# Chunked gated linear attention before two MLPs: a different order of work in each chunk, and other PSUM banks for three of its products

## The chip, the cores and the metric

The kernel runs on one core of a Trainium2 chip. The metric is device time in microseconds (us) from one launch, the median of several runs. Engines are named as in the profile: PE (TensorE matmul), PEld (its weight loads), DVE (VectorE), ACT (ScalarE), POOL (GpSimd), SP (SyncE, which issues all DMAs here).

## The reference

Three stages on float32 data with batch B=4, sequence S=768, model width 384 (8 heads of 48):

```python
f = sigmoid(f_logit)                       # gate per head, token and key channel
state = f[t] * state + k[t] outer v[t]     # per batch and head, 48 x 48
y[t]  = q[t] @ state                       # attention output, 768 tokens
x  = y with heads joined                   # (4, 768, 384)
u  = x + ((x.T @ U) @ V).T                 # token mixing of rank 32
x2 = u + relu(u @ w_ch1) @ w_ch2           # first MLP, 384 -> 1536 -> 384
h  = relu(x2 @ w_in)                       # second MLP, 384 -> 1024
out = (h * sigmoid(conv3(h))) @ w_out      # depthwise conv over the tokens, kernel 3
```

The weights arrive as 64-bit floats and are converted on the chip.

## The kernel before

**Attention.** The recurrence is computed in 24 chunks of 128 tokens, six for each batch. For chunk g, `gate_max(g)` (POOL from chunk 4 on) and `gates(g)` (two ACT passes, exp and ln, in tile `sp`) give the log gates. `prefix(g)` sums them over the tokens with a triangular matmul into tile `n` (PSUM bank 6). ACT makes `a` = exp(-n) and `b` = exp(n) from it; `qh` = q*a and `kh` = k*min(b, limit) follow on POOL (the latter in the inner function `k_hat`). `transposes(g)` turns `qh` and `kh` (banks 1 and 0) and ACT copies them to `qT` and `kT`. `scores(g)` multiplies them into `s` (banks 2 and 3), `mask` applies the causal mask on DVE (tiles `p0`, `p1`). `out_chunk(g)` adds the products `y<-qT,w` (query times state) and `y<-p,v` in bank 4, then forms the chunk's own state product `kv` in bank 7. `state_end(g)` folds `kv` into the running state `w` (DVE `wtmp`, POOL `w`) with the chunk's last gate row, which goes through DRAM (`ends`, `ends_back`).

**Back to tokens and token mixing.** `out_evac(g)` (ACT) copies `y` to `u32`, which is laid out by channel. `tokens(g)` transposes it back to tokens into tile `xt`, also in bank 4; ACT casts it to `xh`, DVE computes the rest `xl` from `xt` and `xh`. `mix_in` adds both into `z` (bank 5). Once a batch is complete, `mix_z` and six calls of `mix_out` (a matmul into a tile `mix` of bank 7 or 6, then a DVE addition into `u32`, row `u`) follow, spread over the chunks of the next batch: in a batch's chunks 3, 4, 5 and, for the batch after, 0, two where the chunk's number i is odd, else one.

**Weight conversion in the gaps.** A weight piece is loaded as raw 64-bit words (`raw`, two buffers), converted in five DVE steps (lines 114 to 118; tiles `cvt`, `cvg`), cast on ACT and completed by a subtraction on POOL. `stage()` issues the load of the next piece, `slot(n)` runs the next n steps. The first pieces are U, the two halves of V (rows `raw<-in_moe_V`), and the convolution weights; 12 pieces of the first MLP's weights follow.

**Order.** The schedule is written out by hand (`manual_schedule`): each engine executes its instructions in program order, and the tile framework adds the waits. A tile in a bank waits for the last reader of the tile that was there before. In each iteration i of the chunk loop PE gets `s(i)`, `n(i+2)`, `z(i-2)`, `xt(i-1)`, the transposes of `qh(i+1)` and `kh(i+1)`, `mix`, `y(i)`, `kv(i)`. DVE gets `wtmp(i-1)`, three conversion steps, both masks, `xl(i-1)`, two conversion steps, `u`. ACT gets the copy of `y(i-1)`, exp and ln of `gates(i+3)`, a weight cast, `a(i+2)`, `xh(i-1)`, `b(i+2)`, the copies of `qT(i+1)`, `kT(i+1)`. POOL gets `w(i-1)`, the weight subtraction, `qh(i+2)`, `b`, `kh(i+2)` and `gate_max(i+4)`. In the first three iterations `gates` runs at the iteration's end. SP issues the loads of `k`, `q`, `f`, `v`, then `ends_back`, one raw piece and `ends`.

**MLPs.** After chunk 23 two MLPs run on PE with each operand split in a high and a low part; the rest of the weight pieces is converted meanwhile. The program ends with a branch on a flag (`tc.If`, line 846) to a fallback that is not taken in these runs.

Of the kernel before, what the change touches and what calls it, by code (L numbers as in the profile page):

```python
# [9 lines left out]
F32 = mybir.dt.float32  # L10
F32R = mybir.dt.float32r
I32 = mybir.dt.int32
# [3 lines left out]

DECAY_LIMIT = 40.0
N_EARLY = 12
SLOT = (3, 2)
EARLY_GATES = 4  # L20
WARM_UP = (8, 5)
FILL_FROM = 22
O_BUFS = 6
SPLIT_FROM = 3
# [7 lines left out]
def kernel(  # L32
# [60 lines left out]

    def w64_load(pool, pairs, p, n):
        raw = pool.tile([128, 2 * 384], I32, tag="raw", name="raw")
        for r0, r1, shape, src in pairs:
            dst = raw[r0:r1, 0:2 * n]
            if shape:  # L100
                dst = dst.rearrange("p (a x) -> p a x", a=shape)
            nc.sync.dma_start(out=dst, in_=src)
        return raw, p, n
# [47 lines left out]
    def mlps(ms, banks, pieces, late, extra):  # L151
# [234 lines left out]
        while done < len(units):  # L386
            down2(*units[done][1:])
            done += 1
            yield

# [12 lines left out]
    def bank(i, shape, name):  # L405
        return banks.tile(shape, F32, tag=f"k{i}", name=name)
# [13 lines left out]

    def heads(t):
        return t.rearrange("p a (j x) -> p (a j) x", j=2)[:, :, 0:D]

    ft, qt, kt, vt = {}, {}, {}, {}
    sps = {}
# [55 lines left out]
    def ends(g):  # L481
        nc.sync.dma_start(out=ends_d[g], in_=a_t[g % 3][127:128].rearrange("o p d -> o (p d)"))
# [4 lines left out]

    qT, kT, sc, pt = {}, {}, {}, {}

    def transposes(g):  # L490
        for src, dst, nm in ((q_t[g % 2], qT, "qT"), (k_t[g % 3], kT, "kT")):
            ps = bank(0 if nm == "kT" else 1, [MP, NP, C], nm + "p")
            for p in range(NP):
                nc.tensor.transpose(out=ps[:, p, :], in_=src[:, p, 0:MP], identity=ident)
            t = (wk1 if nm == "kT" else wk2).tile([MP, NP, C], F32, tag=nm, name=nm)
            nc.scalar.copy(out=t, in_=ps)
            dst[g] = t

    def scores(g):
        kk, qq = kT.pop(g), qT[g]  # L500
# [8 lines left out]
    def mask(g, j):  # L509
        t = wk1.tile([128, NP, C], F32, tag=f"p{j}", name=f"p{j}")  # L510
        nc.vector.tensor_tensor(  # L511
            out=t, in0=sc[g][j], in1=tri.unsqueeze(1).to_broadcast([128, NP, C]), op=ALU.mult
        )
        pt[g].append(t)
# [27 lines left out]
    def strips(parts, started):  # L542
        rounds = [[] for _ in range(4)]
        for part in parts:
            rounds[part[0]].append(part)
        while any(rounds):
            for q in rounds:
                if q:
                    c, dst, lhsT, rhs = q.pop(0)
                    mm(dst, lhsT, rhs, c not in started, False)  # L550
                    started.add(c)

    def out_chunk(g):
        yt[g] = ps = bank(4, [128, KD, C], "y")
        qq, vv, pp = qT.pop(g), vt[g], pt.pop(g)
        parts = []

        def add(gr, lhsT, rhs):
            m, c = divmod(gr, 4)
            parts.append((c, ps[32 * c:32 * (c + 1), m, :], lhsT, rhs))  # L560

        if g % NCH:
            w = w_t[g % 2]
            for p in range(NP):
                for x in range(3):
                    add(3 * p + x, w[:, p, 32 * x:32 * (x + 1)], qq[:, p, :])
        for x, gr, j in ((0, 0, 0), (1, 1, 0), (2, 1, 1), (3, 2, 1)):
            for p in range(NP):
                e = 128 * p + 32 * x
                add(3 * p + gr, vv[:, e:e + 32], pp[j][:, p, :])  # L570
        strips(parts, set())
        if (g + 1) % NCH:
            strips(state(g), set())
        vt.pop(g)
# [3 lines left out]
    def out_evac(g):  # L578
        nc.scalar.copy(out=u32[:, :, g * C:(g + 1) * C], in_=yt.pop(g))

    def tokens(g):
        ps = bank(4, [128, DM], "xt")
        for m in range(KD):
            nc.tensor.transpose(out=ps[:, m * 128:(m + 1) * 128], in_=u32[:, m, g * C:(g + 1) * C], identity=ident)
        h_ = wk1.tile([128, DM], F32R, tag="xh", name="xh")
        l_ = wk1.tile([128, DM], F32R, tag="xl", name="xl")
        nc.scalar.copy(out=h_, in_=ps)
        xh[g], xl[g] = h_, l_
        return lambda: sub(nc.vector, l_, ps, h_.bitcast(F32))
# [69 lines left out]
    with tc.manual_schedule():  # L659
# [5 lines left out]
        )  # L665
        nc.vector.memset(one, 1.0)
        nc.vector.memset(ga, 1.0)
        nc.vector.memset(a_t[0], 1.0)
        nc.vector.memset(q_t[0], 0.0)
        nc.vector.memset(k_t[0], 0.0)  # L670
        for t in v_t:
            nc.gpsimd.memset(t[:, 0:NP * 128].rearrange("p (a x) -> p a x", a=NP)[:, :, D:VO], 0.0)
        for t, x in ((q_t[1], 0.0), (k_t[1], 0.0), (a_t[1], 1.0), (k_t[2], 0.0), (a_t[2], 1.0),
                     (w_t[0], 0.0), (w_t[1], 0.0)):
            nc.gpsimd.memset(t, x)
        for dst, src, nm, g in (
            (ft, f_logit, "f", 0), (kt, k, "k", 0), (qt, q, "q", 0), (ft, f_logit, "f", 1),
            (ft, f_logit, "f", 2), (kt, k, "k", 1), (qt, q, "q", 1), (vt, v, "v", 0),
# [61 lines left out]
        mask(0, 0)  # L740
        mask(0, 1)
        gate_max(3)
        transposes(1)
        prefix(2)()
        gates(3)
        slot(5)
        out_chunk(0)
        load(ft, f_logit, "f", 4)
        load(kt, k, "k", 3)
        load(qt, q, "q", 3)  # L750
        load(vt, v, "v", 2)
        load(vt, v, "v", 3)
        ends(1)
        ends(2)
        ends_back(1)
        slot(1)
        for i in range(1, NG):
# [6 lines left out]
                load(vt, v, "v", i + 3)  # L764
            if i + 1 < NG:
                ends_back(i + 1)
            out_evac(i - 1)
            scores(i)
            if i % NCH:
                state_end(i - 1)  # L770
            if EARLY_GATES <= i and i + 3 < NG:
                gates(i + 3)
            follow = slot_end()
            if 1 < i < FILL_FROM:
                slot(SLOT[0])
            mask(i, 0)
            k_hat = prefix(i + 2) if i + 2 < NG else None
            if i > 1:
                mix_in(i - 2)
            x_low = tokens(i - 1)  # L780
            mask(i, 1)
            x_low()
            if k_hat:
                k_hat()
            for step in follow:
                step()
            if i + 1 < NG:
                transposes(i + 1)
            if i < EARLY_GATES:
                gate_max(i + 3)  # L790
                gates(i + 3)
# [5 lines left out]
                ends(i + 2)  # L797
            if i == FILL_FROM + 1:
                next(mlp)
            if i > 1 and (i - 1) % NCH == 0:  # L800
                b = (i - 1) // NCH - 1
                late_work.append(mix_z(b))
                mixq += [(b, x) for x in range(2 * KD)]
            elif (i - 1) % NCH > 1:
                for at in (7, 6) if i % 2 else (7,):
                    if mixq:
                        mix_out(*mixq.pop(0), at)
            out_chunk(i)
            while tail_work:
                tail_work.pop(0)()  # L810
            if i == FILL_FROM + 1:
# [8 lines left out]
            if i == FILL_FROM:  # L820
                assert not (steps or ready or late_work)
                ls.close()
                mlp = mlps(ms, banks, wq, late, extra)
                next(mlp)
        while mixq:
            mix_out(*mixq.pop(0))
        out_evac(NG - 1)
        mix_in(NG - 2)
        tokens(NG - 1)()
        next(mlp)  # L830
# [170 lines left out]
```

## Time and profile before

| what | us |
|---|---|
| median of 3 runs (lowest to highest) | 678.66 (678.36 to 680.11) |
| the profiled execution, its own time | 681.33 |
| its span, first to last instruction | 679.6 |
| attention, chunk 0's scores to the first MLP matmul | 12.9 to 167.5 |
| busy over the span: PE, DVE, ACT, POOL | 648.3, 441.5, 278.1, 168.4 |

Busy time of PE counts matmuls that wait in its pipeline, so a share near 100% does not say that nothing can be gained. A time in a row is counted from the span's start. The mean granted TensorE clock is 0.993 of full speed.

### The profile page before, as it was taken

What the parts mean: (1) busy time and instruction counts of PE and PEld (TensorE: products, weight loads), DVE (VectorE), ACT (ScalarE), POOL (GpSimd) and SP (SyncE); (2) the same over time, 40 slices, a digit from 0 to 9 for tenths busy, and PEclk for the clock granted to TensorE, in tenths of its full rate; (3) what the DMA queues carried; (4) which work ended last, traced back from release to release, by engine and by line L of the source; (5) the groups of instructions that cost most, each with busy time, mean ns of one, the idle gap of its engine ahead of it and who ended that gap; (6) DMA issues with size and microseconds to landing.
All of it is one profiled execution on the core that took longest, in us unless ns stands there. A gap on an engine that the chain in (4) does not pass through costs nothing.

```text
span 679.6 us, 13505 instructions
## 1 busy us (share of the span) xinstructions
PE 648.3 (95%) x5564; PEld 621.7 (91%) x5564; DVE 441.5 (65%) x697; ACT 278.1 (41%) x554; POOL 168.4 (25%) x202
## 2 busy tenths in 40 slices
PE   7869898989999999999999999999999999999996
PEld 6767777778999999999999999999999999999995
DVE  5658989966899786666211241114898787777763
ACT  5647777764332232123111221113544644553542
POOL 2646778774132131113000020002020120120000
PEclk9979999999999999999999999999999999999999
DMA  8788898841143222210000000000000100100102
GB/s 177 144 163 178 173 202 175 167 84 49 48 139 94 71 70 70 55 62 1 1 0 1 1 1 1 0 1 2 0 1 1 70 1 0 70 1 1 69 1 75
DMA packets 126922, 41.18 MB, mean 61 GB/s; under 512 B 113300, under 2 KB 124076, under 8 KB 126852
## 3 DMA queue, kind: packets, MB, share of 16 engines
q1 hardware_dynamic: 126852, 40.24, 25.3%
q8 instruction: 45, 0.74, 0.4%
q14 instruction: 25, 0.20, 0.1%
HBM read 35.46 MB, written 4.77 MB: 59 GB/s over the span
## 4 chain that ended last, share of the span: by engine, by line
PE 71%; DVE 14%; POOL 4%; ACT 3%; issue 3%; DMA 2%; SPq 2%; POOLq 0%; DVEq 0%; ACTq 0%
PE a L69 33%; PE b L69 32%; PE y L69 3%; DVE cvt L115 2%; DMA q<-in_q_dram 2%; DVE cvg L118 2%; DVE cvg L117 1%; DVE cvt L116 1%; POOL qh L463 1%; DVE cvt L114 1%; PE s L69 1%; DVE p L511 1%; SPq L438 1%; DVE rl L206 1%; DVE xl L72 1%
## 5 line engine op out<-in xcount | busy, mean ns | idle before, releaser
L206 DVE SCALAR_TENSOR_TENSOR rl<-a,rh 128x384 fp32r<-128x384 f32 x96 | 52.6, 556 | 138.3 <-ACT rh L202 138.0
L202 ACT ACTIVATE rh<-a 128x384 fp32r<-128x384 f32 x96 | 47.2, 492 | 219.4 <-PE a L69 219.4
L69 PE MATMUL a<-uh,w1h 128*128 128x384 f32 x288 | 96.6, 336 | 1.0 <-DVE rl L206 1.0
L69 PE MATMUL a<-ul,w1h 128*128 128x384 f32 x288 | 96.6, 335 | 0.0
L69 PE MATMUL b<-rh,w2h 128*128 128x384 f32 x288 | 96.3, 334 | 0.0
L69 PE MATMUL a<-uh,w1l 128*128 128x384 f32 x288 | 96.2, 334 | 0.0
L69 PE MATMUL b<-rh,w2l 128*128 128x384 f32 x288 | 96.2, 334 | 0.0
L69 PE MATMUL b<-rl,w2h 128*128 128x384 f32 x288 | 96.2, 334 | 0.0
L72 POOL TENSOR_TENSOR ul<-u,uh 128x384 fp32r<-128x384 f32 x18 | 23.0, 1298 | 196.2 <-ACT uh L91 196.2
L69 PE MATMUL b<-woh,w1h 128*128 128x384 f32 x264 | 70.9, 337 | 0.0
L69 PEld LDWEIGHTS a<-uh,w1h 128*128 128x128 f32 x288 | 54.1, 188 | 1.9 <-DVE rl L206 1.7
L69 PEld LDWEIGHTS a<-ul,w1h 128*128 128x128 f32 x288 | 54.1, 188 | 0.6 <-DVE ul L72 0.6
L256 ACT ACTIVATE c<-c 128x768 f32<-128x768 f32 x31 | 26.3, 848 | 69.2 <-DVE c L286 69.2
L69 PEld LDWEIGHTS b<-rh,w2h 128*128 128x128 f32 x288 | 54.1, 188 | 0.3 <-issue 0.2
L69 PEld LDWEIGHTS a<-uh,w1l 128*128 128x128 f32 x288 | 54.1, 188 | 0.0
L69 PEld LDWEIGHTS b<-rl,w2h 128*128 128x128 f32 x288 | 54.1, 188 | 0.0
L69 PEld LDWEIGHTS b<-rh,w2l 128*128 128x128 f32 x288 | 54.1, 188 | 0.0
L69 PE MATMUL a<-w2h,winh 128*128 128x384 f32 x192 | 48.8, 335 | 0.0
L69 PEld LDWEIGHTS b<-woh,w1h 128*128 128x128 f32 x264 | 48.1, 188 | 0.0
L69 PE MATMUL b<-wol,w1h 128*128 128x384 f32 x132 | 44.4, 336 | 0.0
L248 ACT ACTIVATE h<-a 128x384 f32<-128x384 f32 x64 | 30.4, 495 | 24.3 <-PE a L69 24.0
L280 DVE TENSOR_SCALAR c<-h,cw 128x768 f32<-128x768 f32 (+1 forms) x33 | 24.2, 734 | 22.8 <-ACT h L248 22.7
(129 smaller groups left out, 1381.1 us busy)
## 6 DMA issues: line engine op xcount, KB each, us to landing
raw<-in_moe_w_ch_dram SPq DMA_DIRECT2D x24, 384.0 KB, 3.1
f<-in_f_logit_dram SPq DMA_DIRECT2D x24, 192.0 KB, 4.9
k<-in_k_dram SPq DMA_DIRECT2D x24, 192.0 KB, 3.2
q<-in_q_dram SPq DMA_DIRECT2D x24, 192.0 KB, 4.6
v<-in_v_dram SPq DMA_DIRECT2D x48, 96.0 KB, 3.4
out_dram<-o SPq DMA_DIRECT2D x24, 192.0 KB, 1.9
raw<-in_moe_w_in_dram SPq DMA_DIRECT2D x8, 384.0 KB, 3.3
raw<-in_moe_w_out_dram SPq DMA_DIRECT2D x8, 384.0 KB, 3.4
```

The costliest lines, as they stand in the source:

```text
L69: nc.tensor.matmul(out=out, lhsT=lhsT, rhs=rhs, start=start, stop=stop, skip_group_check=True)
L72: eng.tensor_tensor(out=out, in0=a, in1=b, op=ALU.subtract)
L114: lambda: ve.tensor_scalar(out=t, in0=hi, scalar1=3, scalar2=0x3FFFFFFF, op0=ALU.logical_shift_left, op1=ALU.bitwise_and),
L115: lambda: ve.scalar_tensor_tensor(out=t, in0=hi, scalar=-(1 << 30), in1=t, op0=ALU.bitwise_and, op1=ALU.bitwise_or),
L116: lambda: ve.scalar_tensor_tensor(out=t, in0=lo, scalar=29, in1=t, op0=ALU.logical_shift_right, op1=ALU.bitwise_or),
L117: lambda: ve.tensor_scalar(out=g, in0=hi, scalar1=0x7FF00000, scalar2=None, op0=ALU.bitwise_and),
L118: lambda: ve.scalar_tensor_tensor(out=w, in0=g, scalar=LEAST_NORMAL, in1=t.bitcast(F32), op0=ALU.is_ge, op1=ALU.mult),
L202: nc.scalar.activation(out=rh[:, hf], in_=ps, func=ACTF.Relu)
L206: nc.vector.scalar_tensor_tensor(out=rl[:, hf], in0=ps, scalar=0.0, in1=rh[:, hf].bitcast(F32), op0=ALU.max, op1=ALU.subtract,)
L248: nc.scalar.activation(out=h[:, 1 + hf.start:1 + hf.stop], in_=ps, func=ACTF.Relu)
L256: nc.scalar.activation(out=c, in_=c, func=ACTF.Sigmoid)
L280: nc.vector.tensor_scalar(out=c[:, s], in0=h[:, t0 + 1:t1 + 1], scalar1=cw[:, J2 + jc[0]:J2 + jc[0] + 1], scalar2=None, op0=ALU.mult)
```

## The change

- `tokens` writes `xt` into bank 0; the transposes of `qh` and `kh` share bank 1 (new function `turn`).
- In each iteration the order is: `state_end(i-1)`, `prefix(i+2)` (PE `n`, ACT `a`, POOL `qh`), `scores(i)`, `k_hat` (ACT `b`, POOL `b`, `kh`), `gates(i+3)`, two conversion steps, `mix_in`, both masks, `tokens(i-1)`, the turn of `qh(i+1)`, `xl`, three conversion steps, `mix_out` (now bank 6), `out_chunk(i)`, `out_evac(i)`, a second `mix_out` in bank 0 where i is odd, and last the turn of `kh(i+1)`.
- One more call of `stage()` ahead of the loop: each raw piece is fetched one piece earlier, with three buffers for `raw` until the MLPs begin. The second half of V is then issued behind the loads that follow chunk 0.
- At the start only the columns between the heads are filled in the `qh`, `kh` and `a` tiles (`between`); the two `w` tiles are filled by DVE instead of POOL. Seven warm-up matmuls instead of eight before the first prefix.
- After the last product of the second MLP, 16 matmuls are issued whose result nobody reads.

```diff
-SLOT = (3, 2)
+SLOT = (2, 3)
-WARM_UP = (8, 5)
+WARM_UP = (7, 5)
...
+    raw_bufs = [3]
-        raw = pool.tile([128, 2 * 384], I32, tag="raw", name="raw")
+        raw = pool.tile([128, 2 * 384], I32, tag="raw", name="raw", bufs=raw_bufs[0])
...
+        flat = w2h.rearrange("p j x -> p (j x)")
+        ps = [bank(i, [128, 512], "wide") for i in range(2)]
+        for n, turns in ((512, 1), (384, 1), (384, 2), (256, 1)):
+            for i in range(4):
+                mm(ps[i % turns][:, 0:n], flat[:, 128 * i:128 * (i + 1)], flat[:, 0:n], turns > 1 or i == 0, False)
...
+    def between(t):
+        return t.rearrange("p a (j x) -> p (a j) x", j=2)[:, :, D:64]
...
+    def turn(g, nm):
+        src, dst = (q_t[g % 2], qT) if nm == "qT" else (k_t[g % 3], kT)
+        ps = bank(1, [MP, NP, C], nm + "p")
+        for p in range(NP):
+            nc.tensor.transpose(out=ps[:, p, :], in_=src[:, p, 0:MP], identity=ident)
+        t = (wk1 if nm == "kT" else wk2).tile([MP, NP, C], F32, tag=nm, name=nm)
+        nc.scalar.copy(out=t, in_=ps)
+        dst[g] = t
...
     def tokens(g):
-        ps = bank(4, [128, DM], "xt")
+        ps = bank(0, [128, DM], "xt")
...
-        nc.vector.memset(a_t[0], 1.0)
-        nc.vector.memset(q_t[0], 0.0)
-        nc.vector.memset(k_t[0], 0.0)
+        for t, x in ((a_t[0], 1.0), (q_t[0], 0.0), (k_t[0], 0.0)):
+            nc.vector.memset(between(t), x)
+        for t in w_t:
+            nc.vector.memset(t, 0.0)
...
-        transposes(1)
+        turn(1, "qT")
...
         out_chunk(0)
+        out_evac(0)
+        turn(1, "kT")
...
         load(vt, v, "v", 3)
+        stage()
         ends(1)
...
-            out_evac(i - 1)
-            scores(i)
             if i % NCH:
                 state_end(i - 1)
+            k_hat = prefix(i + 2) if i + 2 < NG else None
+            scores(i)
+            if k_hat:
+                k_hat()
...
-            mask(i, 0)
-            k_hat = prefix(i + 2) if i + 2 < NG else None
             if i > 1:
                 mix_in(i - 2)
+            mask(i, 0)
+            mask(i, 1)
             x_low = tokens(i - 1)
-            mask(i, 1)
+            if i + 1 < NG:
+                turn(i + 1, "qT")
             x_low()
-            if k_hat:
-                k_hat()
...
-            if i + 1 < NG:
-                transposes(i + 1)
...
+            late_mix = []
...
-                for at in (7, 6) if i % 2 else (7,):
-                    if mixq:
-                        mix_out(*mixq.pop(0), at)
+                if mixq:
+                    mix_out(*mixq.pop(0), 6)
+                if mixq and i % 2:
+                    late_mix.append(mixq.pop(0))
             out_chunk(i)
+            out_evac(i)
+            for m in late_mix:
+                mix_out(*m, 0)
+            if i + 1 < NG:
+                turn(i + 1, "kT")
...
+                raw_bufs[0] = 2
...
-        out_evac(NG - 1)
```

## Rows read from the trace of the kernel before

**Rows 1.** Windows between `scores`: length, busy PE, PEld, DVE, ACT, POOL, clock, DMA share.
```profile
30.16:43.46 13.30, 7.41 (x127) 6.50 (x120) 4.32 (x9) 5.48 (x12) 5.19 (x9) 0.81 0.83 163
...
50.27:74.48 24.21, 21.42 (x429) 18.02 (x422) 21.45 (x39) 18.76 (x42) 17.10 (x23) 1.00 0.87 178
74.48:112.15 37.67, 34.27 (x671) 28.27 (x665) 34.44 (x62) 26.84 (x58) 29.12 (x38) 1.00 0.88 184
112.15:118.92 6.77, 6.30 (x129) 5.06 (x122) 6.57 (x12) 4.62 (x10) 4.97 (x7) 1.00 0.88 187
118.92:125.12 6.20, 5.82 (x129) 4.87 (x121) 5.30 (x10) 3.66 (x9) 5.21 (x7) 1.00 0.69 149
125.12:130.88 5.76, 5.74 (x97) 4.64 (x89) 5.37 (x11) 4.04 (x9) 4.85 (x7) 1.00 0.85 169
130.88:136.42 5.54, 5.29 (x100) 4.18 (x96) 4.87 (x9) 4.72 (x10) 3.68 (x6) 1.00 0.88 177
136.42:142.61 6.19, 5.57 (x127) 4.74 (x120) 5.44 (x10) 4.65 (x11) 4.33 (x6) 1.00 0.90 167
142.61:149.85 7.24, 5.56 (x127) 4.77 (x119) 3.72 (x7) 5.17 (x12) 5.80 (x8) 1.00 0.32 49
149.85:167.53 17.68, 16.57 (x333) 14.04 (x327) 12.66 (x27) 8.49 (x19) 8.48 (x12) 1.00 0.16 47
```

**Rows 2.** Waits of PE, 0 to 215 us: total, times, longest.
```profile
PE y L69 <- DVE xl L72: 10.3, 11, 5.0
PE y L69 <- POOL qh L463: 5.5, 5, 1.7
```

**Rows 3.** Timeline of chunks 2 and 3, all engines.
```profile
27.57 1.00 POOL L463 TENSOR_TENSOR qh<-q,a 128x384 f32<-128x384 f32 x1 [2.36 <-DMA q<-in_q_dram]
...
32.17 0.91 PE L69 MATMUL n<-sp,tri 128*128 128x384 f32 x2 [0.85 <-ACT sp L454]
...
33.42 1.37 SPq L102 DMA_DIRECT2D raw<-in_moe_V_dram  x3
...
36.59 0.57 DVE L114 TENSOR_SCALAR cvt<-raw 96x384 int32<-96x384 int32 x1 [5.47 <-DMA raw<-in_moe_V_dram]
...
39.68 1.51 PE L69 MATMUL y<-qT,w 112*32 112x128 f32 x24 [5.04 <-DVE xl L72]
```

**Rows 4.** Groups of POOL instructions, chunks 9 to 20: busy, mean ns.
```profile
L469 POOL TENSOR_TENSOR kh<-k,b 128x384 f32<-128x384 f32 x12 | 13.2, 1099 | 1.0
...
L467 POOL TENSOR_SCALAR b<-b 128x384 f32<-128x384 f32 x12 | 7.3, 612 | 1.0
```

**Rows 5.** Timeline of the start, all engines.
```profile
3.69 1.88 DVE L446 TENSOR_SCALAR sp<-f 128x384 f32<-128x384 f32 x1 [1.00 <-DMA f<-in_f_logit_dram]
...
20.84 1.00 POOL L463 TENSOR_TENSOR qh<-q,a 128x384 f32<-128x384 f32 x1 [0.39 <-DMA q<-in_q_dram]
```

**Rows 6.** Timeline of chunk 1's prefix sums and the ACT instructions behind them.
```profile
11.99 0.91 PE L69 MATMUL n<-sp,tri 128*128 128x384 f32 x2 [0.17 <-ACT sp L454]
...
13.00 0.49 ACT L462 ACTIVATE a<-n 128x384 f32<-128x384 f32 x1
...
14.89 0.58 ACT L496 COPY qT<-qTp 112x512 f32<-112x512 f32 x1
```

**Rows 7.** Groups of DVE instructions, chunks 9 to 20: busy, mean ns.
```profile
L118 DVE SCALAR_TENSOR_TENSOR cvg<-cvg,cvt 128x384 f32<-128x384 int32 x10 | 8.2, 822 | 0.3
...
L72 DVE TENSOR_TENSOR xl<-xt,xh 128x384 fp32r<-128x384 f32 x12 | 6.6, 551 | 2.1 <-ACT xh L587 1.9
...
L117 DVE TENSOR_SCALAR cvg<-raw 128x384 int32<-128x384 int32 x9 | 5.0, 559 | 0.1
```

**Rows 8.** The end: chain that ended last, then line 846's semaphore instructions.
```profile
660.50 12.51 PE b L69 x72
...
L846 SPq EVENT_SEMAPHORE  x8: 17/17/17, 677.5 to 678.2; - x8
...
L846 PEldq EVENT_SEMAPHORE  x1: 51/51/51, 673.9 to 673.9; - x1
```

More of the change, by code (lines that the diff above doesn't have):

```diff
@@ L488 @@
     qT, kT, sc, pt = {}, {}, {}, {}
-    def transposes(g):
[L491 to L497, printed above, removed]
+    def turn(g, nm):
[6 more added lines that the diff above has]
+        dst[g] = t
+    def transposes(g):
+        turn(g, "qT")
+        turn(g, "kT")
     def scores(g):
@@ L555, in out_chunk, with part @@
         qq, vv, pp = qT.pop(g), vt[g], pt.pop(g)
-        parts = []
-        def add(gr, lhsT, rhs):
+        started = set()
+        def part(gr, lhsT, rhs):
             m, c = divmod(gr, 4)
-            parts.append((c, ps[32 * c:32 * (c + 1), m, :], lhsT, rhs))
+            return c, ps[32 * c:32 * (c + 1), m, :], lhsT, rhs
         if g % NCH:
             w = w_t[g % 2]
[L564 to L571, printed above, removed]
+            strips([part(3 * p + x, w[:, p, 32 * x:32 * (x + 1)], qq[:, p, :])
+                    for p in range(NP) for x in range(3)], started)
+        strips([part(3 * p + gr, vv[:, 128 * p + 32 * x:128 * p + 32 * (x + 1)], pp[j][:, p, :])
+                for x, gr, j in ((0, 0, 0), (1, 1, 0), (2, 1, 1), (3, 2, 1)) for p in range(NP)], started)
         if (g + 1) % NCH:
@@ L667 @@
         nc.vector.memset(ga, 1.0)
-        nc.vector.memset(a_t[0], 1.0)
-        nc.vector.memset(q_t[0], 0.0)
-        nc.vector.memset(k_t[0], 0.0)
+        for t, x in ((a_t[0], 1.0), (q_t[0], 0.0), (k_t[0], 0.0)):
+            nc.vector.memset(between(t), x)
+        for t in w_t:
+            nc.vector.memset(t, 0.0)
         for t in v_t:
             nc.gpsimd.memset(t[:, 0:NP * 128].rearrange("p (a x) -> p a x", a=NP)[:, :, D:VO], 0.0)
-        for t, x in ((q_t[1], 0.0), (k_t[1], 0.0), (a_t[1], 1.0), (k_t[2], 0.0), (a_t[2], 1.0),
-                     (w_t[0], 0.0), (w_t[1], 0.0)):
-            nc.gpsimd.memset(t, x)
+        for t, x in ((q_t[1], 0.0), (k_t[1], 0.0), (a_t[1], 1.0), (k_t[2], 0.0), (a_t[2], 1.0)):
+            nc.gpsimd.memset(between(t), x)
         for dst, src, nm, g in (
```

## The prediction

> **What bounds the kernel now.** I read the windows first, cut at each start of `scores` [rows 1]. The attention stage is PE's, but with gaps: chunks 15 to 20 take 6.77, 6.20, 5.76, 5.54, 6.19 and 7.24 us, while PE is busy 5.3 to 6.3 us in each. Chunk 3 alone takes 13.30 us, at a mean clock of 0.81. In chunks 9 to 14 DVE is busy 34.44 of 37.67 us and the DMA engines 0.88 of the time, so two other resources stand close behind PE. Chunk 20 (7.24 us) has DVE busy only 3.72: not DVE's load but a chain of waits costs 1.68 us there (7.24 - 5.56).
>
> The waits [rows 2] name the chain: `y` stood behind `xl` for 10.3 us, and 5.5 us more are put down to POOL `qh`, which `y` doesn't read and which runs at about the time of `xl`; I count them with `xl`. `y(i)` takes bank 4 from `xt(i-1)`, and `xl` is `xt`'s last reader. Then the timeline of chunk 3 [rows 3]: V's second half is issued at 33.42, DVE waits 5.47 us for it, the masks and `xl` queue behind, and PE stands 5.04 us before `y`.
>
> After 167.5 us the MLPs keep PE filled until 673 us; nothing of their order changes. An earlier end of attention moves them as a whole.
>
> **The change, part by part.**
>
> *V earlier, chunks 1 to 4.* DVE's wait of 5.47 us goes. What is late next is the loop through the gates: `n` first in each iteration means that `s(i)` now queues on PE behind an `n(i+2)` that, in iterations 1 to 3, waits for `gates(i+2)`, ended late in the iteration before. Before, the scores ran ahead of that wait. V's three issues (1.37 us [rows 3]) also move ahead of chunk 4's loads on SP, so q(4), which POOL already waited 2.36 us for until 27.57, comes at about 28.9. From there: `qh` 1.0, `b` 0.6, `kh` 1.1 [rows 4], `gate_max` 0.5 (taken as a little under `b`), exp and ln 1.15 (an estimate, the larger part of the 1.89 in which ACT starts and works off `a`, `b`, exp and ln [rows 6]): `n(5)` at 33.3 instead of 32.17, and chunk 3's scores 0.8 behind it at 34.1 instead of 30.16. The same loop gives the next `n`: 0.95 from `n` to `a`, 0.49, 1.0, 0.6, 1.1, 0.5, 1.15, and some 0.5 of hand-offs make 6.3, so `n(6)` at 39.6 and chunk 4's scores at 40.5 (43.46 before). From chunk 4 on `gates` is out of this loop. Chunk 4 then takes 5.6 (PE's work in a chunk without mixing is 5.57 [rows 1]) instead of 6.81 (43.46 to 50.27): scores of chunk 5 at 46.1. **Gain 4.2.** Bounds: 0 if the loads of q(5), q(6), f(7) come as late as before and everything waits for them; 8.3 if chunk 3 takes 6.2 and chunk 4 5.6.
>
> *The start.* The first `gate_max` takes 1.88 us on DVE while POOL fills tiles [rows 5]; shorter fills can give 1.3 of it back. But `qh(3)` at 20.84 waits for its q load, whose place on SP doesn't change. I take 0, and 1.3 as the other bound. One warm-up matmul less is inside that wait: 0.
>
> *Chunks 5 to 8* (24.21 us, no mixing yet). `y` no longer waits for `xl`; PE's busy 21.42 is the lower bound. The DMA share 0.87 would pass 0.93 at 22.6, and DVE has 21.45 of work. **Gain 1.0**, bounds 0 and 2.5.
>
> *Chunks 9 to 19.* Two things oppose each other. Without the wait for `xl`, a batch's chunk 1 goes from 6.19 to 5.5, chunk 2 from 7.2 to 6.3 (5.56 of PE's work and some 0.7 in which `y<-p,v` waits for masks, since DVE comes late from the first step of `mix_z`): -0.7, -0.7, -0.9 for chunks 13, 19 and 14. But `mix` now always takes bank 6, whose next tile is `n(i+3)`, first on PE in the next iteration, and its reader `u` is DVE's last instruction of the iteration: behind `n` queue `s`, `z`, `xt`, `y` on PE and `a`, `b`, the gates and `xh` on ACT. The loop is: `u` to `n` 0.1; `n` 0.91 and a hand-off to `a`, 0.95; ACT until the gates are done 1.89 [rows 6]; a weight cast in five of six iterations, as long as `a`, 0.4 in the mean; `xh` 0.49; `xl` 0.55; on average 2.5 conversion steps (the sixth place in six is the cast's) of 0.56 to 0.82, taken as 0.64, 1.6; `u` 0.55 like `xl` [rows 7]. Sum 6.53, taken as 6.5. It closes eight times (chunks 9 to 12 and 15 to 18), where the mean was (6.77 + 6.20 + 5.76 + 5.54)/4 = 6.07 [rows 1]: +3.4. **Net +1.1.** Bounds: -5 if DVE reaches `u` before PE is ready for `n` in every chunk (then PE's work decides: 34.3 against 37.7 a batch), +5 if each loop takes 7.0.
>
> *Chunks 20 to 23.* No conversion steps remain, so the loop is short. Chunk 20 falls from 7.24 to 5.7; in 21 to 23 PE is idle 1.1 of 17.68, nearly all before `y`, of which 0.9 goes. **Gain 2.4**, bounds 0.5 and 3.
>
> *The end.* The 16 matmuls come after PE's last product, which ends at 673.0 [rows 8]. By the pitch of the 384-column products before them (72 in 12.51, 0.17 us each; the wider ones more, the narrower less) they take about 2.8 us. PE's semaphore instruction of line 846 is at 673.9, SP's at 677.5: 3.6 us of cover. I take 0; without the cover they would cost 2.8.
>
> Sum: -4.2 - 1.0 + 1.1 - 2.4 = -6.5. The profiled execution took 681.33 (span 679.6 and 1.7 around it), 2.7 above the median of the runs; it would be 674.8. Against the median of 678.66 this gives **672.2 us**.
>
> **A rule weighed against the rows.** The step L118, which reads two SBUF tiles, takes 0.82 us in the mean against 0.56 of L117, which reads one [rows 7], so something stretches it. The Trainium skill, page "SBUF — State Buffer", section "SBUF: two separate sides", says that DVE and GpSimd share one pair of SBUF ports under an exclusive lock: whoever starts first holds it for the whole instruction, and the other waits. Its price here is that of the second rival below.
>
> **The rivals.**
>
> *PE's floor* (0.18). If `u` is always done before `n` is due, chunks 9 to 19 gain 5 instead of losing 1.1, and with 2 for chunks 5 to 8 the sum is -4.2 - 2 - 5 - 2.4 = -13.6: 665. For it: PE idles 3.4 us a batch, and those waits are what the change moves. Against it: DVE's 34.44 of 37.67.
>
> *Slower* (0.13): the three conversion steps that now stand between `xl` and `u` meet POOL's `kh` and weight subtraction, 1.1 us each. If each step waits out one of those, three steps last 3.3 instead of 1.6, the loop 8.2, and eight loops cost 17 instead of 3.4: -6.5 + 13.6 gives 685.8. It becomes slower than now by 0.3% once a loop takes 7.55. For it: L118's mean; against it: L117's mean, and that POOL has other work in between. The skill's rule, taken for every step, gives this 685.8.
>
> *No change* (0.15): the gates' loop keeps chunks 1 to 4 at the pace of the loads (gain 0 to 1), and the rest is as forecast (+1.1, -1.0, -2.4) or, with the bounds of chunks 5 to 8 and of the end, up to 3 worse: 676 to 680.
>
> **How the numbers follow.** The forecast, 667 to 676.5, gets 0.54. A measurement of this kernel can tell about 0.3%, 2 us, from no change. Faster: 0.54 + 0.18 = 0.72; same 0.15; slower 0.13. Of the first rival the nearer half lies above 665.5, and to 679.5 reaches most of no change; beyond these ends lie about 0.09 and 0.11. The range is 665.5 to 679.5.
>
> **What would show it.** Right: chunk 3 under 8 us and no DVE wait for V; PE waiting for ACT `sp` before `n(4)` to `n(6)`; no wait of `y` for `xl`; PE waiting for DVE `u` before `n` in the eight mixing chunks, with loops near 6.5 us; chunk 20 under 6. Wrong: no waits before these `n`, and chunks at 5.6 to 5.8 throughout (floor); waits of 1 us and more there, with conversion steps over 1 us (slower); line 846's semaphores on SP later after the last output copy than before (the end not hidden).

## The result, and the profile after

The changed kernel takes 686.76 us in the median of four runs (685.14 to 689.83), the kernel before 679.18 beside it. The ratio is 1.0116, with a 95% interval of 1.0077 to 1.0156: slower by about 1.2%, where 1% faster was forecast. The profiled execution took 687.48 us, its span 685.8 (679.6 before).

Lengths of chunks, here and below, run from the start of one `scores` to the next in the timeline. The 6.2 us of span, stretch by stretch, from the two traces:

| stretch | before | after | difference | forecast |
|---|---|---|---|---|
| span's start to scores of chunk 5 | 50.27 | 47.26 | -3.0 | -4.2 |
| chunks 5 to 8 | 24.21 | 24.44 | +0.2 | -1.0 |
| chunks 9 to 19 | 68.13 | 75.49 | +7.4 | +1.1 |
| chunk 20 | 7.24 | 5.69 | -1.55 | -1.5 |
| chunk 21 to the first MLP product | 17.43 | 20.62 | +3.2 | -0.9 |
| first MLP product to the span's end | 512.3 | 512.3 | 0 | 0 |

The first MLP product before is that of 167.28. In the traces of all versions below the last stretch takes 510.7 to 515.2 us, so 1 or 2 us there can't be read from one trace.

Windows of the changed kernel, columns as in [rows 1]:
```profile
17.51:26.63 9.12, 5.61 (x118) 4.35 (x117) 5.55 (x11) 4.23 (x9) 5.39 (x8) 0.99 0.70 140
26.63:35.35 8.72, 8.70 (x120) 7.10 (x119) 4.15 (x9) 4.04 (x8) 3.54 (x6) 0.62 0.91 169
...
47.26:71.70 24.44, 22.57 (x421) 17.57 (x421) 19.22 (x37) 19.34 (x41) 16.24 (x21) 1.00 0.88 181
...
71.70:80.21 8.51, 6.73 (x122) 5.14 (x122) 8.31 (x16) 3.96 (x8) 5.55 (x9) 1.00 0.99 216
80.21:87.88 7.67, 7.55 (x121) 5.93 (x121) 6.20 (x12) 4.43 (x9) 6.07 (x8) 0.78 0.93 191
87.88:94.25 6.37, 5.92 (x91) 4.54 (x90) 5.69 (x11) 4.23 (x9) 4.98 (x6) 1.00 0.90 189
...
111.93:120.39 8.46, 6.72 (x121) 5.13 (x121) 8.27 (x16) 4.00 (x8) 5.50 (x9) 1.00 0.75 154
120.39:128.01 7.62, 6.03 (x121) 4.79 (x120) 6.72 (x12) 4.23 (x9) 6.03 (x8) 1.00 0.89 180
128.01:135.29 7.28, 7.25 (x90) 5.67 (x90) 5.69 (x11) 4.43 (x9) 4.63 (x6) 0.77 0.52 98
147.19:152.88 5.69, 5.66 (x120) 4.61 (x120) 3.81 (x8) 5.16 (x11) 4.49 (x6) 1.00 0.25 32
152.88:173.50 20.62, 16.39 (x323) 13.46 (x324) 12.98 (x28) 8.96 (x19) 8.46 (x12) 0.99 0.13 41
```
Chunk 9 takes 8.51 us with DVE busy for 8.31 of them, chunk 15 is like it. Chunk 10 has PE busy throughout, but at a mean clock of 0.78; so has chunk 17 (0.77), and chunk 2 (0.62). Chunk 16, the same place in the next batch as chunk 10, takes 7.62 us at a clock of 1.00: in that place the lower clock costs next to nothing. Chunk 20, where no conversion and no mix is left, is as short as forecast.

Waits of PE, then of its weight loads (PEld), in the changed kernel, 0 to 215 us, as in [rows 2]:
```profile
PE n L69 <- DVE u L634: 6.9, 6, 1.6
PE n L69 <- ACT sp L464: 3.9, 2, 3.5
...
PE a L69 <- DVE xl L72: 1.2, 1, 1.2
```
```profile
PEld s L69 <- ACT kT L506: 11.5, 17, 1.0
PEld n L69 <- DVE u L634: 8.7, 7, 1.8
```
The wait of `y` for `xl` is gone. In its place PE stands before `n`, for `u`; its weight loads stand before `s`, for `kT`, 17 times; and the first MLP product waits for `xl`.

DVE on its way into chunk 9 and through it (timeline):
```profile
71.04 1.24 DVE L118 SCALAR_TENSOR_TENSOR cvt<-raw,cvt 128x384 int32<-128x384 int32 x1
72.21 0.66 DVE L119 TENSOR_SCALAR cvg<-raw 128x384 int32<-128x384 int32 x1
72.90 0.56 DVE L120 SCALAR_TENSOR_TENSOR cvg<-cvg,cvt 128x384 f32<-128x384 int32 x1
73.37 0.73 DVE L549 TENSOR_TENSOR wtmp<-kv,w 48x192 f32<-48x192 f32 x2
...
75.76 0.55 DVE L72 TENSOR_TENSOR xl<-xt,xh 128x384 fp32r<-128x384 f32 x1
...
78.77 1.01 DVE L634 TENSOR_TENSOR u<-mix,u 128x384 f32<-128x384 f32 x2
```
The first three are steps of iteration 8, which end 1.8 us into chunk 9 (it starts at 71.70). So DVE comes to `xl` 2.0 us after ACT has begun `xh` (73.76), where 0.5 passes in chunk 10.

One closed loop, from the `n` of iteration 10 to the next (timeline, DVE, ACT and PE rows):
```profile
79.36 0.91 PE L69 MATMUL n<-sp,tri 128*128 128x384 f32 x2 [1.54 <-DVE u L634]
...
80.31 0.49 ACT L472 ACTIVATE a<-n 128x384 f32<-128x384 f32 x1 [1.87 <-PE n L69]
...
82.15 0.50 ACT L91 CAST w1h<-cvg 128x384 fp32r<-128x384 f32 x1
83.12 0.48 ACT L597 CAST xh<-xt 128x384 fp32r<-128x384 f32 x1 [0.48 <-PE xt L594]
...
83.64 0.56 DVE L72 TENSOR_TENSOR xl<-xt,xh 128x384 fp32r<-128x384 f32 x1 [0.71 <-ACT xh L597]
84.11 0.35 DVE L116 TENSOR_SCALAR cvt<-raw 128x384 int32<-128x384 int32 x1
84.50 1.25 DVE L117 SCALAR_TENSOR_TENSOR cvt<-raw,cvt 128x384 int32<-128x384 int32 x1
85.78 0.74 DVE L118 SCALAR_TENSOR_TENSOR cvt<-raw,cvt 128x384 int32<-128x384 int32 x1
86.44 0.54 DVE L634 TENSOR_TENSOR u<-mix,u 128x384 f32<-128x384 f32 x1
```
POOL in the same stretch:
```profile
83.17 1.00 POOL L479 TENSOR_TENSOR kh<-k,b 128x384 f32<-128x384 f32 x1
84.13 1.19 POOL L72 TENSOR_TENSOR w1l<-cvg,w1h 128x384 fp32r<-128x384 f32 x1
```
It is the loop that the prediction drew: `n`, ACT's row up to `xh`, `xl`, three conversion steps, `u`, and then the next `n`. It takes 7.67 us here instead of 6.5: from `a` to `xh` 2.8 instead of 2.3 (`xh` waits 0.48 for `xt`, which PE computes at the lower clock), and from `xl` to `u` three steps of 2.33 instead of 1.6; the step of 84.50 lasts 1.25 us while POOL's weight subtraction (84.13 to 85.32) runs beside it. (Lines have moved by two: L116 to L120 are the five steps, so that L118 is now the third of them and no longer the fifth, as in the prediction.)

The hand-over to the MLPs, timeline of PE:
```profile
171.85 0.49 PE L594 MATMUL xt<-ident,u 128*128 128x128 f32 x3
173.50 0.69 PE L69 MATMUL a<-uh,w1h 128*128 128x384 f32 x1 [1.16 <-DVE xl L72]
173.99 0.52 PE L69 MATMUL a<-ul,w1h 128*128 128x384 f32 x1
...
176.55 0.34 PE L69 MATMUL a<-uh,w1h 128*128 128x384 f32 x1
```
The MLPs' first product takes bank 0, where the last `xt` now is. It waits 1.16 us, and the next eight products are paced at 0.32 us instead of 0.17: the lower of the two clock levels (1.2 instead of 2.4 GHz). All waits of PE from the scores of chunk 21 to that product:
```profile
PE s L69 <- ACT kT L506: 1.5, 2, 0.7
PE a L69 <- DVE xl L72: 1.2, 1, 1.2
PE gp L835 <- DVE g L833: 0.8, 1, 0.8
PE y L69 <- POOL w L550: 0.8, 2, 0.6
```
They are 4.3 us, against 1.1 before (`y` for `xl`, twice): that is the 3.2 of the table.

### The profile page after: what moved, and what is told of

It reads as the page before. It is cut to its first block, busy times and chain, and to the rows that moved or that the text cites. A ratio compares the mean times of both kernels' runs of the same rounds, so it can differ in the third digit from the quotient of the medians.

```text
span 685.8 us, 13558 instructions
## 1 busy us (share of the span) xinstructions
PE 658.3 (96%) x5578; PEld 624.1 (91%) x5578; DVE 438.1 (64%) x699; ACT 280.1 (41%) x554; POOL 168.9 (25%) x200
## 4 chain that ended last, share of the span: by engine, by line
PE 84%; DVE 7%; ACT 4%; POOL 2%; issue 2%; DMA 1%; SPq 0%; ACTq 0%; POOLq 0%; DVEq 0%
PE a L69 36%; PE b L69 35%; PE y L69 3%; PE s L69 3%; PE n L69 2%; PE z L69 1%; PE kTp L504 1%; DMA f<-in_f_logit_dram 1%; PE qTp L504 1%; DVE cvt L117 1%; PE xt L594 1%; ACT sp L464 1%; DVE p L525 1%; DVE cvt L118 1%; DVE xl L72 1%
## 5 line engine op out<-in xcount | busy, mean ns | idle before, releaser
L525 DVE TENSOR_TENSOR p<-s,tri 128x512 f32<-128x512 f32 x48 | 30.9, 686 | 13.9 <-PE s L69 13.7
```

What stands on the lines that cost most here:

```text
L525: nc.vector.tensor_tensor(out=t, in0=sc[g][j], in1=tri.unsqueeze(1).to_broadcast([128, NP, C]), op=ALU.mult)
```

## The experiments

The losses that the trace suggests were first undone one at a time. The ratios are to runs of the kernel before on the same chip, with 95% intervals.

**Mixes late** (nothing stands in `n`'s bank when `n` comes).
```diff
-                if mixq:
-                    mix_out(*mixq.pop(0), 6)
-                if mixq and i % 2:
-                    late_mix.append(mixq.pop(0))
+                for at in (0, 4) if i % 2 else (0,):
+                    if mixq:
+                        late_mix.append((*mixq.pop(0), at))
```


> The changed kernel, but every mixing product comes after out_chunk, in bank 0 (and a second one in bank 4), so that no `u` stands before an `n`. First theory (the new n waits for u through bank 6, and this is where chunks 9 to 19 lose their time): no wait of PE for u before n, chunks 9 to 19 fall from 75.5 us to 66 to 69, the whole to 677 to 680. Rival (the new order itself costs, because conversion steps are stretched against GpSimd wherever the products stand): chunks 9 to 19 stay above 73 us, the whole at 684 to 687.

Measured 685.2 (1.0078, 1.0050 to 1.0107). The wait of `n` for `u` is gone, and chunks 9 to 19 take 71.25 instead of 75.49, but 3.1 more than before remain. PE now waits for DVE and POOL elsewhere (`y` for `w` and for the masks). Chunks 5 to 8 and 21 to 23 of this trace were 0.6 and 0.9 longer, which took back part of the gain; by the medians, whose intervals overlap, it can't be told from the changed kernel.

**The last `xt` in bank 4.**
```diff
-        ps = bank(0, [128, DM], "xt")
+        ps = bank(0 if g + 1 < NG else 4, [128, DM], "xt")
```


> The changed kernel, but chunk 23 alone is transposed back in bank 4, so that the first MLP product (bank 0) needs no xl. Theory that the hand-over costs: the 1.16 us wait and the slow first products go, and the whole is 1 to 2.6 us shorter than the changed kernel. Rival (VectorE sets the pace of the first MLP's start and takes the gain back): under 0.5 us shorter.

Measured 684.1 (1.0068, 1.0048 to 1.0087); the first MLP product comes at 170.94 instead of 173.50 and takes 0.42 us. Of these 2.6 us 1.0 stem from chunks 5 to 8, whose code is the same; chunk 21 to the first product takes 19.19 instead of 20.62, 1.4 less. The eight products at half pace had cost 1.2 more (8 times 0.15). So the hand-over is worth some 2.6 us, and the medians differ by 2.7.

**V early alone**: the kernel before with only three raw buffers and the earlier `stage()`.
```diff
+    raw_bufs = [3]
-        raw = pool.tile([128, 2 * 384], I32, tag="raw", name="raw")
+        raw = pool.tile([128, 2 * 384], I32, tag="raw", name="raw", bufs=raw_bufs[0])
...
+        stage()
         ends(1)
```


> The kernel before, with only the earlier fetch of the raw pieces (three buffers, one more call of stage). If VectorE's wait for V was on the path: chunk 3 falls from 13.3 to about 8 us and the whole by 4 to 6 us, to 673 to 675. Rival (the loads of q and f behind V's three issues come later and hold the gates' chain): 677 to 679, with longer waits of GpSimd for q.

Measured 677.0 (0.9955, 0.9938 to 0.9973). Chunk 3 falls from 13.30 to 7.99, the scores of chunk 5 start at 45.78: earlier than in the changed kernel (47.26). This part alone makes the kernel faster, and the rest of the change takes more than it gives.

**Three conversion steps ahead of the masks, two behind**, as before the change.
```diff
-SLOT = (2, 3)
+SLOT = (3, 2)
```


> The changed kernel with three conversion steps before the masks and two behind xl, as before the change. First theory (n waits for u): each of the eight mixing loops is one step shorter, 0.6 to 1.2 us, so the whole is 4 to 8 us shorter than the changed kernel. Rival (VectorE's work sets the pace, whatever its order): the masks come later by the same step, and the whole stays within 1.5 us of the changed kernel.

Measured 682.1 (1.0025, 1.0001 to 1.0049). Chunks 9 to 12 take 7.93, 7.04, 6.36, 5.21 instead of 8.51, 7.67, 6.37, 6.31, and chunks 9 to 19 70.3. One step less in the loop is worth 5 us over the batches.

**Both transposes in one bank, in the order of before** (V early, `xt` in bank 0, transposes of queries and keys both in bank 1).
```diff
-            ps = bank(0 if nm == "kT" else 1, [MP, NP, C], nm + "p")
+            ps = bank(1, [MP, NP, C], nm + "p")
...
-        ps = bank(4, [128, DM], "xt")
+        ps = bank(0 if g + 1 < NG else 4, [128, DM], "xt")
```


> The kernel before with two parts of the change: V early with three raw buffers, and the bank part (both transposes of a chunk in bank 1, xt in bank 0, the last xt in bank 4). The order of prefix sums, gates, masks, mixes and keys' transposes is that of before. Theory 'the order costs, the banks pay': y no longer waits for xl, chunks 13, 14, 19 and 20 fall from 6.2, 7.2, 6.2 and 7.2 us to 5.6, 6.3, 5.6 and 5.7; the median is 673 to 675, 2 to 4 below V early alone (677.0). Theory 'DVE bounds chunks 9 to 19 in any order': only chunk 20 falls, and the median is 675.5 to 677.

Measured 688.9 (1.0128, 1.0093 to 1.0162). Both theories fell. Its waits of PE, 0 to 215 us:
```profile
PE kTp L496 <- ACT qT L498: 24.6, 20, 2.8
```
The keys' transposes follow the queries' directly and need their bank, so PE stands before them 1.2 us a chunk until ACT has copied `qT`. With a shared bank the keys' transposes have to stand elsewhere in the order.

**Late mixes, three steps and bank 4 together**, the edits of the runs above.

> The changed kernel with all three cures of the earlier runs together: mixes late in banks 0 and 4 (alone 685.2), three conversion steps ahead of the masks and two behind (alone 682.1), the last xt in bank 4 (alone 684.1), against 686.8 for the changed kernel. If the three losses are separate, the gains add: -1.5 -4.7 -2.7 gives 678, no different from the kernel before. If late mixes and the moved step cure the same wait of n for u, the larger one and the hand-over remain: 679 to 681.

Measured 684.9 (1.0089, 1.0064 to 1.0114): the gains don't add. With the mixes late the two `u` come after `y`, and with three steps ahead of the masks `y` waits for `p` (2.1 us in chunk 18, which takes 8.93 at a clock of 0.82). The order has little slack: what is taken out of one wait stands in the next.

**PE kept busy in its waits**: matmuls that nobody reads behind the keys' transposes of five iterations.
```diff
+            if i in FILL:
+                ps = bank(4, [128, NP, C], "fill")
+                for x in range(FILL[i]):
+                    mm(ps[:, x % NP, :], tri, tri, True, True)
```


> The changed kernel with 25 extra matmuls of 128 columns (tri by tri, into bank 4, read by nobody) behind the keys' transposes of iterations 9, 12, 15, 16 and 18, where PE then stands 0.7 to 1.6 us waiting for u: PE works in the wait, nothing else moves. If the granted clock falls because PE stood still, s in the next chunk takes 1.16 instead of 1.41 us, the window that follows has a clock above 0.95 instead of 0.78, and chunks 9 to 19 shrink by 1 to 2.5 us of 75.5. If the lower clock costs nothing because DVE sets the loop, the clock rises and the chunks keep their lengths within 0.3 us. If the clock has another cause, neither moves.

Measured 685.3 (1.0093, 1.0060 to 1.0125). Its windows of chunks 9, 10 and 17:
```profile
71.12:79.97 8.85, 8.07 (x134) 6.53 (x134) 8.66 (x16) 3.93 (x8) 5.89 (x9) 1.00 0.95 208
79.97:87.57 7.60, 6.02 (x121) 4.78 (x121) 6.71 (x12) 4.23 (x9) 6.00 (x8) 1.00 0.93 192
...
127.72:134.08 6.36, 5.93 (x90) 4.53 (x90) 5.68 (x11) 4.23 (x9) 4.97 (x6) 1.00 0.62 120
```
The clock stays at 1.00, and chunk 10 keeps its length (7.60 against 7.67): a slow PE costs next to nothing there. Only chunk 17 falls, from 7.28 to 6.36. Of the 7.4 us lost in chunks 9 to 19 the clock is about 0.9. That the extra matmuls kept the clock up is not shown: in the next run, which has none, PE stood 1.57 to 1.59 us before four `n` of chunks 9 to 19, the clock of chunks 10 and 17 was 1.00 all the same, and they took 7.61 and 6.37.

**Scores ahead of the prefix sum in iterations 1 to 3.**
```diff
+            if i < EARLY_GATES:
+                scores(i)
             k_hat = prefix(i + 2) if i + 2 < NG else None
-            scores(i)
+            if i >= EARLY_GATES:
+                scores(i)
```


> The changed kernel, but in iterations 1 to 3 the scores are issued ahead of the prefix sum again, as before the change. If the loop through the gates with n at its head costs the early chunks, PE no longer stands 3.5 us before n(4) with the scores behind it, and the scores of chunk 5 start at about 45.8 us as with V early alone, instead of 47.3; the median is 685.3. If the loads of f and q set the early chunks, the start of chunk 5 stays within 0.4 us of 47.3.

Measured 689.2 (1.0154, 1.0118 to 1.0190), and the scores of chunk 5 start at 50.63: 3.4 later, so neither theory held. With the keys' transposes last, `s` waits for `kT` (3.2 us in iteration 2), and `n`, now behind `s`, waits with it.

**Banks apart.** `xt` goes to bank 7 (that of `kv`, which `y` doesn't touch); queries' and keys' transposes keep a bank each; `mix` goes to 6 and 1. Once with V early in the order of before:
```diff
-        ps = bank(4, [128, DM], "xt")
+        ps = bank(7, [128, DM], "xt")
...
-                for at in (7, 6) if i % 2 else (7,):
+                for at in (6, 1) if i % 2 else (6,):
```


> The kernel before with V early, and xt out of y's bank in another way than in the changed kernel: xt takes bank 7 (that of kv, which y doesn't touch), queries' and keys' transposes keep a bank each (1 and 0), mixes take banks 6 and 1. Order as before. Theory 'the bank of y was the wait that counted, the shared bank of both transposes and the new order spoilt it': waits of y for xl are gone, chunks 13, 14, 19 and 20 fall from 6.2, 7.2, 6.2 and 7.2 to 5.6, 6.3, 5.6 and 5.7, the median is 673 to 675 (V early alone 677.0). Theory 'the wait for xl only hid the wait for the masks, DVE comes late anyway': y waits for p in its place, chunks stay within 0.2 us, the median is 676.5 to 678.

Measured 675.9 (0.9919, 0.9904 to 0.9933). PE's wait of `y` for `xl` is gone; what remains before `y` is 0.9 us for the masks in three places. Chunks 13, 14, 19 and 20 take 5.50, 6.71, 5.49 and 6.94. The wait for `xl` was real (0.9919 against 0.9955 for V early alone), but chunks 9 to 19 shrink only from 68.1 to 67.4. And once in the changed order, with the keys' transposes beside the queries' (`turn(i + 1, "kT")` right behind `turn(i + 1, "qT")`, bank 0) and the mixes behind `y` in banks 1 and 0:

> The changed kernel (prefix sums first) with the banks of the run beside it: xt in bank 7, keys' transposes in bank 0 right behind the queries', ahead of y instead of last, mixes behind y in banks 1 and 0. Theory 'keys last costs': s no longer stands for kT (11.5 us in the changed kernel), n never for u; chunks 9 to 19 fall from 75.5 to about 68, and the median comes to 678 to 680. Theory 'n first costs by itself, since gates and masks follow it': the chunks stay at 71 and more as with late mixes alone, the median is 683 to 686.

Measured 679.0 (0.9974, 0.9955 to 0.9994); chunks 9 to 19 take 69.8. With nothing shared that is read late, the changed order is no longer slower than the kernel before, but slower than the old order with `xt` and the transposes in the same banks. The mixes' banks, the start and the matmuls at the end differ too, so that the difference isn't the order's alone.

**Three steps, bank 4, and no extra matmuls at the end.**

> The changed kernel with three conversion steps ahead of the masks and two behind (alone 682.1), the last xt in bank 4 (alone 684.1 against 686.8) and without the 16 extra matmuls at the end. If the two losses are separate, 682.1 - 2.7 gives 679.4, and if the extra matmuls cost what the end of the span grew by (0.35), 679.0. If they cost their whole 2.8, 676.6. In the profile: last product to the end of the span 6.6 us if the extra matmuls matter, 6.95 if not.

Measured 680.5 (0.9984, 0.9970 to 0.9999). From PE's last useful product to the span's end 8.6 us pass here without the 16 matmuls (in the slowest of eleven executions), 6.95 with them in the changed kernel, 6.6 in the kernel before. Over all nineteen traces it is 5.9 to 7.9 with them and 6.6 to 8.6 without: they cost nothing that can be seen.

**The start** (shorter fills, one warm-up matmul less) added to the faster of the two versions with banks apart: the fills and `WARM_UP` of the change's diff.

> The version of the last call with the order of before, V early and xt in bank 7 (675.9 there), and in addition the start of the changed kernel (shorter fills, w's fills on DVE, one warm-up matmul less). The first scores start at 11.7 to 11.9 us instead of 12.9, as in the changed kernel. If that is kept, the median falls by 1 to about 674.8 and is the fastest here; if POOL's wait for q at 20 us takes it back, as the prediction had it, the scores of chunk 2 start within 0.3 us of 23.2 and the median stays at 675.9.

Measured 674.6 (0.9926, 0.9900 to 0.9952; the kernel before took 679.8 beside it and 681.3 beside the version without the start). The first scores start at 10.90 instead of 12.94, those of chunk 5 at 44.40 against 44.27: all of it is taken back. By the ratios the two versions can't be told apart.

**PE kept busy before n(4)**, in the changed order with banks apart. A first attempt put the 16 matmuls into bank 4; they had to wait there for ACT's copy of `y`, which stood behind the gates, and ran after the wait instead of in it (682.0; 1.0027, 1.0007 to 1.0047). In bank 0:
```diff
+            if i == 1:
+                ps = bank(0, [128, NP, C], "fill")
+                for x in range(16):
+                    mm(ps[:, x % NP, :], tri, tri, True, True)
```


> The version with xt in bank 7 and the changed order (679.0) with 16 extra matmuls at the end of iteration 1, now in bank 0, which is free there (in bank 4 they had to wait for ACT's copy of y, which stands behind the gates on ACT, and came after the wait instead of into it). If the standing PE lowers the clock, the chunk behind n(4) runs at 1.00 instead of 0.70 and the scores of chunk 4 start 1 to 2.5 us before 42.05, the median is 677 to 678. If the loads set the early chunks, they start within 0.5 us of 42.05 whatever the clock.

Measured 679.5 (0.9972, 0.9949 to 0.9995). Timeline of PE:
```profile
21.80 3.84 PE L69 MATMUL fill<-tri 128*128 128x128 f32 x32
25.77 0.91 PE L69 MATMUL n<-sp,tri 128*128 128x384 f32 x2
26.61 1.16 PE L69 MATMUL s<-qT,kT 48*128 48x128 f32 x16
...
40.06 1.16 PE L69 MATMUL s<-qT,kT 48*128 48x128 f32 x16
```
The clock of chunk 2 is 1.00 (0.70 without the filler), `n` takes 0.91 (1.65), and the scores of chunk 4 start at 40.06 instead of 42.05. From the start of n(4) to these scores 14.29 us pass instead of 15.97, so in these two traces the lower clock behind n(4) cost some 1.7 us. The median doesn't show it: chunk 23 was 1.3 longer in this trace.

**Each part of the order alone**, added to the version of 674.6 us. Scores ahead of the prefix sum in the version that has it first (`scores(i)` above `prefix(i + 2)`) had given 683.5 (1.0050, 1.0031 to 1.0068):

> The same version with the changed order, but the scores ahead of the prefix sum in every iteration (the one part of the order that is put back). If 'prefix sums first' is what the order costs (24.7 against 23.7 us in chunks 20 to 23, 69.8 against 67.4 in chunks 9 to 19, scores of chunk 5 at 47.7 against 44.3), the scores of chunk 5 start by 45.5, chunks 9 to 19 take 67.5 to 68.3, and the median is 676 to 677. If masks together, gates' place or late mixes cost it, chunks 9 to 19 stay at 69.5 to 70 and the median at 678 to 679.5.

This fell: putting that one part back made things worse, since `xt` and `kv` then waited in its stead. So the parts were added instead. Prefix sums first:
```diff
+            k_hat = prefix(i + 2) if i + 2 < NG else None
             scores(i)
...
             mask(i, 0)
-            k_hat = prefix(i + 2) if i + 2 < NG else None
...
-                for at in (6, 1) if i % 2 else (6,):
+                for at in (1, 0) if i % 2 else (1,):
```


> The fastest version so far (674.6: order of before, V early, xt in bank 7, the start of the change) with one part of the changed order: the prefix sum, its exponential and qh at the head of each iteration, the scores behind them; mixes in banks 1 and 0, so that none stands in n's bank. If 'prefix sums first' costs by itself, through the scores that queue behind gates early and through ACT's order later, the scores of chunk 5 start 1.5 to 3 us later than 44.4, chunks 9 to 19 take 69 instead of 67.3, and the median is 677 to 679. If it costs nothing once the banks are apart, the median is 674 to 675.5.

Measured 681.1 (1.0005, 0.9977 to 1.0033 against 0.9926): about 5 us lost. `n` waits for the gates 7.6 us in five places (4.6 in four without the part), and the scores of chunk 5 start at 49.36 instead of 44.40, of which chunks 5 to 8 take 2.4 back. Mixes that follow ACT's copy of `qT` in bank 1 add 5.3 us of waits. So the 5 us are those of the order and of the mixes' new banks together; the run doesn't separate them. Keys' transposes last:
```diff
-                transposes(i + 1)
+                transposes(i + 1, ("qT",))
...
             out_chunk(i)
+            if i + 1 < NG:
+                transposes(i + 1, ("kT",))
```


> The fastest version so far (674.6) with another part of the changed order: the keys' transposes behind y and kv instead of beside the queries', in their own bank 0. The next scores then stand for ACT's copy of kT, 0.6 to 0.7 us a chunk as in the changed kernel. If that is on the path, 19 chunks from 5 on cost 0.3 to 0.6 each, 6 to 11 in all, and the median is 680 to 686. If PE's slack before the scores and DVE's lateness hide it, the median stays at 674 to 676.

Measured 692.1 (1.0172, 1.0099 to 1.0244 against 0.9926): about 17 us lost, more than the whole change. Its timeline at the start of chunk 14:
```profile
106.52 0.65 PE L500 MATMUL kTp<-ident,kh 128*112 128x128 f32 x4
107.21 0.58 ACT L502 COPY kT<-kTp 112x512 f32<-112x512 f32 x1 [0.84 <-PE kTp L500]
...
107.84 0.38 PE L69 MATMUL s<-qT,kT 48*128 48x128 f32 x2 [0.67 <-ACT kT L502]
```
PE has nothing between `kTp` and the scores, so ACT's copy lies bare; PE stands 18.4 us before `s` in all, against 2.3 without the part. In the changed kernel `n` stands in that place and covers it, for the price of `n` waiting for `u` and for the gates.

## Why the prediction was wrong, point by point

By the table, forecast and measurement lie 12.7 us apart: 6.3 of them in chunks 9 to 19, 4.0 in chunks 20 to 23, 1.2 each in chunks 0 to 4 and 5 to 8.

**Chunks 9 to 19 (+1.1 forecast, +7.4 measured): the step that failed is the size of the mixing loop.** The waits came where the prediction put them: `mix` in bank 6, `n` behind `u`, ACT's row and `xl` in between; the run with late mixes removed the wait and 4.2 us. But the eight loops took 8.51, 7.67, 6.37, 6.31, 8.46, 7.62, 7.28 and 6.22, a mean of 7.3 and not 6.5. Three of them are even below the forecast; what makes the 6.2 us is this:

- Chunks 9 and 15, 3.9 us: DVE is full there (8.31 of 8.51, 8.27 of 8.46), since it enters them with steps of the iteration before. So `xl` comes 2.0 us after `xh` has begun, not 0.5, and DVE's own row sets the length instead of the chain through ACT. The sum let DVE reach `xl` as soon as `xh` is there, and a mean over the batch hid these chunks.
- The conversion steps were taken at 0.64 us each, for 2.5 of them. Where three stand between `xl` and `u` (chunks 9, 10, 15, 16) they took 2.3 to 2.9. In chunks 10 and 16 this makes most of 2.2 us; the two steps of chunks 11, 12 and 18 took 1.6, as in the sum.
- The lower clock cost chunk 17 0.9 us (against 6.37 in chunk 11, the same place at a clock of 1.00).

A likely reason why the old order could bear a full chunk is that its next scores don't wait for `u`, so that a full chunk can borrow from a slack one; with `n` at the head of the next chunk it can't. No run shows this by itself.

The rival "slower" had named the place and the sign, waits of 1 us and more with steps over 1 us, and its time (685.8) is near the measured one. That is luck in part: it needed loops of 8.2, with each step waiting out a POOL instruction. With the measured mean of 7.3 its sum gives 678.4, no change; the rest of the loss came from terms that it took over from the forecast. In the changed kernel L118 takes 0.56 us at most in the five cases where no POOL instruction runs beside it, and 1.24 or 1.25 in the four beside `kh` or a weight subtraction; beside `qh`, which starts after it in both cases, it keeps 0.56. The rule of the Trainium skill, page "SBUF — State Buffer", section "SBUF: two separate sides" (an exclusive lock between DVE and GpSimd, held by whoever starts first), fits these rows; it is met by one or two steps of a loop, not by all.

**Keys' transposes last and the shared bank: not costed at all.** The prediction counted neither the wait of `s` for `kT` (11.5 us of weight loads' waits after, in chunks 22 and 23, where no `n` stands between, 0.73 us each on PE) nor that the moved transposes, the shared bank and "prefix sums first" hang together. Alone, keys last costs 17 us; prefix sums first with the mixes in banks 1 and 0 costs 5; the shared bank with `xt` in bank 0, without the reordering, costs 12 (1.0128 against 0.9955 for V early alone).

**Chunks 20 to 23 (-2.4 forecast, +1.6 measured).** Chunk 20 came as forecast, 5.69. For the rest the prediction took a wait of 0.9 us away and put the new waits at nothing. There are 4.3 us of them: 1.5 of `s` for `kT`, 1.2 at the hand-over, where the last `xt` has moved to the bank of the MLPs' first product, and 0.8 each of `y` for the state `w` and of `gp`, a transpose for the branch flag, for a reduction that DVE reaches behind `u`. With the half-speed products behind it the hand-over cost 2.6 us. With only the loops put right, the forecast's sum gives no change (678.4); with these 4.0 us as well it is already slower (682.4).

**V earlier (-4.2 forecast, -3.0 measured): right, the term 1.2 too large.** The wait for V is gone, and the forecast times of chunk 3's, 4's and 5's scores (34.1, 40.5, 46.1) are each passed by 1.1 to 1.3 us (35.35, 41.57, 47.26). PE stood 3.5 us before n(4), as foreseen; not foreseen was that the following chunk then ran at a clock of 0.62. In the sister version with the filler in that wait, chunk 4's scores came 2.0 us earlier, 1.7 of it behind n(4).

**Chunks 5 to 8 (-1.0 forecast, +0.2 measured).** `y` no longer waits for `xl`, yet nothing was won. One trace says little here: with the same code in this stretch the changed kernel, the last `xt` in bank 4 and the scores ahead in iterations 1 to 3 took 24.4, 23.5 and 23.4. V early alone, both versions with banks apart, the one with the start and the changed kernel reach chunk 5 at anything from 44.3 to 47.7 us and chunk 9 at 70.4 to 71.7, with the DMA engines busy 0.88 to 0.93 of the time in chunks 5 to 8. That the loads set this stretch is argued from that, not shown by a run of its own.

**The start and the end (0 and 0): right.** The start's gain of 2 us is gone by chunk 5, as the prediction had it, and the extra matmuls are covered.

## What to carry to other kernels

A tile that changes its bank gets a new neighbour in time: for every move, list who writes that bank next on an in-order engine and what stands behind that writer, here `n` behind `u`, `kTp` behind `qT`, and the MLPs' first product behind the last `xt`. A mean over iterations is no price for a loop that ties one iteration's end to the next one's start: add up the fullest iteration by itself, with what it takes over from the one before (chunks 9 and 15 took 8.5 where the mean gave 6.5). And a reordering whose parts cover each other (`n` over ACT's copy of `kT`) can be judged neither by one part nor by the whole: what paid here, V early and `xt` apart from `y`, needed none of it (0.9919, and 0.9926 with the start).

## What the runs showed of the hardware

The granted clock fell after PE had stood still, but not each time. In the changed kernel the chunk behind a wait of 3.51 us ran at 0.62, those behind waits of 1.54 and 1.59 us at 0.78 and 0.77, and that behind one of 1.55 us at 1.00 (chunk 16); in the run with the scores ahead in iterations 1 to 3 chunks 10 and 17 ran at 1.00 behind waits of 1.57 and 1.59 us. The Trainium skill, page "TensorE: Matmul & The Clock Gate", section "HAM oscillation — how this bites in real kernels", tells of a kernel whose TensorE falls to the lower level in its waits for DMA, so that the next piece of work starts slow; the rows agree that such falls stand behind waits, here for other engines. They show besides that the lower clock costs next to nothing where another engine sets the pace (7.67 us at 0.78 in chunk 10, 7.62 at 1.00 in chunk 16), and something where PE itself does (0.9 us in chunk 17, some 1.7 behind n(4)).
